# Windowed attention with a gated feed-forward layer: one unit's outputs and the next unit's scores in one visit to TensorE

## The chip, the cores and the metric

The kernel runs on one core of a Trainium2 chip. Its engines are TensorE (PE in the profile; PEld is its weight load), VectorE (DVE), ScalarE (ACT), GpSimd (POOL) and SyncE (SP), which issues the DMAs. The metric is the device time of one execution in microseconds, lower is better; the time of a kernel is the median of its runs.

## The reference

All in float32. Attention over 8 x 8 heads of 576 tokens with head size 64, each token seeing itself and the 63 tokens before it; then a gated layer over all 4608 tokens.

```python
scores = scale * np.matmul(q, k.transpose(0, 1, 3, 2))
rel = pos[:, None] - pos[None, :]
mask = (rel >= 0) & (rel < 64)
scores = np.where(mask, scores, -1000000000.0)
scores = scores - np.max(scores, axis=-1, keepdims=True)
attn = np.exp(scores)
attn = attn / (np.sum(attn, axis=-1, keepdims=True) + 1e-09)
out = np.matmul(attn, v)
x = out.transpose(0, 2, 1, 3).reshape(4608, 512)
gate = 1.0 / (1.0 + np.exp(-(x @ w_gate)))      # w_gate, w_val: 512 x 1536
y = gate * (x @ w_val) @ w_out                  # w_out: 1536 x 512
```

## The kernel before

The tokens are cut into 12 tiles of 384. A tile's attention is 4 units, one for each pair of heads, and a unit (t, p) goes through three stages, each a short visit to PE between long matmuls:

- `stage_a`, scores: 24 matmul records (12 instructions) of 64x64 weights write the scores of the pair's heads into two PSUM banks `s0` and `s1`. Per head and block, DVE takes masked row minima (L211), ACT the exp (L216), DVE sums up and inverts (L222, L223), and POOL scales (L225, giving `p`).
- `stage_b`: 6 transposes of `p` into two banks `pp` (L233), copied out by ACT as `pT` (L238).
- `stage_c`, outputs: 24 records with 128x64 weights (L248) into one bank `oo`, which ACT copies out as `xf` (L255; for tiles 0 and 1 it is split in two parts instead).

PSUM has 8 banks. Six have names of their own, three for even and three for odd s (`psum(s, i)`), and belong to the feed-forward part; the other two are the pool `ps_a` with tag `a`, which from the third tile on serves `s0`, `s1`, `pp` and `oo` in turn. All these tiles have 384 columns, and a bank holds 512, so a quarter of each stays free.

The feed-forward part has a first stretch (tiles 0 and 1, plain matmuls `up`, in rotating banks `h_bank`, and `down`), beside which the attention of tiles 2 and 3 runs and the weights are converted. Then come phases s = 1 to 5, each for tiles 2s and 2s+1 together, by a Strassen scheme: for k = 0 to 5 and m = 0 (gate), 1 (value) there are 7 `product`s n = 0 to 6, each of 6 matmuls of 384 columns (L438) into bank 0, 1 or 2 of the phase: n = 0 and 4 use bank 0, n = 1, 3 and 5 bank 1, n = 2 and 6 bank 2. Here is what leaves these banks, and lets PE write them again:

- n = 0: ACT copies the bank to `p1` (L449). n = 1: DVE adds `p1` to bank 1, giving `u`. n = 3: DVE forms `u` from bank 1 and `c` from bank 2. n = 5: `c` from bank 1. n = 6: `c` from bank 2 (all L444).
- With m = 0 a gate is made of each `c`, and of bank 0 itself after n = 4: ACT's Relu (L292), Tanh (L293) and Exp (L294), and on DVE an abs (L295) and a product (L297). With m = 1 DVE multiplies by the gates (L476, L481).

Behind n = 2, 4 and 6 a `down` (3 matmuls of 512 columns, L347) of the k before is put in where there is one; k = 0 has none, and the second half of k = 1 hardly any. When the products are done, the second tile's downs follow (`last_tile`). Beside phase s the attention of phase s+1's tiles runs, 8 units; phase 5 has none. Products are numbered by slots, 14 for each k.

What stands where on PE is written by hand: events are put with a time, sorted, and PE keeps that program order (`pe`). The order on DVE, ACT, POOL and SP is set by a scheduler that simulates the program when it is built, and each engine works through its queue in order. `q` and `k` of a unit have one buffer each, `v` two, the weights of the products (`W`) seven, each for two products; all loads are issued by SP.

The times of the stages beside a phase, before (the number is the slot behind which a stage stands):

```python
for n in range(2 * NP):
    for f, d in zip(range(3), (0, 6, 8)):
        fill.setdefault(21 * (n // 2) + (2, 11)[n % 2] + d, []).append((f, *unit(s + 1, n)))
```

Of the kernel before, what the change touches and what calls it, by code (L numbers as in the profile page):

```python
# [26 lines left out]
def attn_ffn(ctx: ExitStack, tc: tile.TileContext, qT, kT, vN, w_gate, w_val, w_out, out):  # L27
# [159 lines left out]

    def stage_a(t, p):
        qt, kt = ld.pop((t, p))
        g0 = order[t] * UT  # L190
# [9 lines left out]
        for h in range(2):  # L200
            if t < 2 and (NP * t + p) % 3 == 2:
                pt = mp.tile([P, TT], F32, name=f"p{h}_{t}_{p}", tag=("hh", "hl")[h], bufs=3)
                pt = pt.rearrange("p (u c) -> p u c", u=UP)
            else:
                pt = ap.tile([P, UP, P], F32, name=f"p{h}_{t}_{p}", tag="p", bufs=4)
            mn = sm.tile([P, UP], F32, name=f"mn{h}_{t}_{p}", tag="mn")
            rs = sm.tile([P, UP], F32, name=f"rs{h}_{t}_{p}", tag="rs")
            for u in range(UP):
                key = [int((g0 + 2 * u + s) % SEQ == 0) for s in range(2)]
                key = tuple(key[::-1] if h else key)  # L210
                nc.vector.tensor_tensor_reduce(out=pt[:, u, :], in0=sc[h][:, u, :], in1=masks[key],  # L211
                                               op0=ALU.add, op1=ALU.min, scale=-SCALE, scalar=3.0e38,
                                               accum_out=mn[:, u:u + 1])
                with table_order() if t < 4 else nullcontext():
                    sums = {} if t < 2 and h else {"accum_out": rs[:, u:u + 1]}
                    exp = nc.scalar.activation(pt[:, u, :], pt[:, u, :], AF.Exp, bias=mn[:, u:u + 1],  # L216
                                               scale=-1.0, **sums)
                if t < 4:
                    chain.append(exp.ins)
            if not sums:  # L220
                nc.vector.reduce_sum(out=rs, in_=pt, axis=mybir.AxisListType.X)
            nc.vector.tensor_scalar_add(out=rs, in0=rs, scalar1=1e-9)  # L222
            nc.vector.reciprocal(out=rs, in_=rs)  # L223
            eng = nc.vector if t == 3 and p % 2 else nc.gpsimd
            eng.tensor_mul(out=pt, in0=pt, in1=rs.unsqueeze(2).broadcast_to([P, UP, P]))  # L225
            st[(t, p, h)] = pt
# [14 lines left out]
    def stage_c(t, p):  # L241
        oo = bank(t, p, "o", f"oo_{t}_{p}").rearrange("p u c -> p (u c)")
        vt = vts.pop((t, p))
        pT = [st.pop((t, p, h)) for h in range(2)]
        for U in range(UT):
            for h in range(2):
                half = (U % 2) ^ h
                pe(nc.tensor.matmul(oo[h * BLK:(h + 1) * BLK, U * BLK:(U + 1) * BLK],  # L248
                                    vt[:, U, h * BLK:(h + 1) * BLK],
                                    pT[h][:, U // 2, half * BLK:(half + 1) * BLK], start=True, stop=True))  # L250
        if t < 2:
            xs[(t, p)] = x_split(oo, f"{t}_{p}", 4 * t + p, nc.vector)
        else:
            xf[(t, p)] = xp.tile([P, TT], F32, name=f"xf_{t}_{p}", tag=f"xf{4 * (t % 2) + p}")
            nc.scalar.copy(xf[(t, p)], oo)  # L255
# [426 lines left out]
```

## Time and profile before

| | before |
|---|---|
| median of 3 runs | 1029.6 us (1028.73 to 1029.66) |
| profiled execution | 1027.79 us, span 1026.0 us |
| granted PE clock, mean | 0.991 |
| busy PE / PEld / DVE / ACT / POOL | 988.4 / 884.8 / 660.3 / 526.3 / 264.5 us |
| DMA | 221.51 MB, mean 216 GB/s |

Busy time is the union of an engine's instructions. Matmuls are pipelined: a matmul's start is measured and its end modelled, so that consecutive ones overlap in the listing, and what a matmul takes of the queue is read from start to start. PE counts matmul records: each fp32 instruction of the attention makes two.

### The profile page before, as it was taken

How to read it: one execution, taken by the hardware profiler on the slowest of the kernel's cores; microseconds unless marked ns; L12 is line 12 of the kernel's file. 1: busy time of each engine (PE TensorE's matmuls, PEld its weight loads, DVE VectorE, ACT ScalarE, POOL GpSimd, SP SyncE). 2: the span in 40 equal slices, each digit the busy share in tenths (PEclk: the TensorE clock that was granted, in tenths of full speed). 3: DMA queues.
4: the chain of work that ended last, by engine and by line, in shares of the span. 5: the costliest groups of instructions: out<-in, count | busy, mean ns of one | idle time of the engine just before them, and what ended most of it. 6: DMA issues, size and time to landing. Idle time of an engine off the chain costs nothing.

```text
span 1026.0 us, 19846 instructions
## 1 busy us (share of the span) xinstructions
PE 988.4 (96%) x6984; PEld 884.8 (86%) x6984; DVE 660.3 (64%) x1810; ACT 526.3 (51%) x1409; POOL 264.5 (26%) x287
## 2 busy tenths in 40 slices
PE   5799999998999999999999999999999999999998
PEld 4688999788899888989988989988989988899996
DVE  6499987836676665666665776676666677344542
ACT  6687976735566544544453654454545544311122
POOL 4200101676762231122113221214112124010100
PEclk8899999999999999999999999999999999999999
DMA  9599985989999733767661776761677662476500
GB/s 302 198 304 376 342 303 189 334 294 342 368 315 329 216 109 111 241 211 223 202 197 34 238 240 199 224 199 49 215 225 212 211 189 84 131 226 195 197 31 32
DMA packets 126244, 221.51 MB, mean 216 GB/s; under 512 B 9409, under 2 KB 82625, under 8 KB 126145
## 3 DMA queue, kind: packets, MB, share of 16 engines
q1 hardware_dynamic: 126144, 220.24, 65.6%
q8 instruction: 56, 0.92, 0.4%
q14 instruction: 44, 0.35, 0.1%
HBM read 178.52 MB, written 41.68 MB: 215 GB/s over the span
## 4 chain that ended last, share of the span: by engine, by line
PE 74%; DMA 7%; DVE 6%; ACT 6%; POOL 3%; issue 3%; SPq 1%; POOLq 0%; DVEq 0%; ACTq 0%
PE pr L438 40%; PE y L347 23%; PE oo L248 3%; PE s L197 3%; PE ph L283 2%; ACT p L216 2%; PE pp L233 2%; DMA hd<-hh 1%; DVE w L122 1%; DMA a<-w32d 1%; DMA w32d<-w 1%; DVE w L124 1%; DMA q<-in_qT_dram 1%; POOL ws L144 1%; DMA out_dram<-yo 1%
## 5 line engine op out<-in xcount | busy, mean ns | idle before, releaser
L438 PE MATMUL pr<-x_T,wt 128*128 128x384 f32 x1440 | 288.3, 340 | 5.1 <-DVE c L444 2.8
L438 PEld LDWEIGHTS pr<-x_T,wt 128*128 128x128 f32 x1440 | 251.0, 188 | 21.1 <-DVE u L444 5.4
L347 PE MATMUL y<-w,hh 128*128 128x512 f32 x804 | 250.6, 392 | 0.3 <-DVE w L144 0.2
L438 PE MATMUL pr<-x_B,wt 128*128 128x384 f32 x1080 | 221.9, 342 | 0.2
L438 PEld LDWEIGHTS pr<-x_B,wt 128*128 128x128 f32 x1080 | 188.7, 188 | 7.9 <-ACT g L293 1.3
L225 POOL TENSOR_TENSOR p<-p,rs 128x384 f32<-128x384 f32 x92 | 79.4, 865 | 406.4 <-DVE rs L223 365.6
L347 PEld LDWEIGHTS y<-w,hh 128*128 128x128 f32 x804 | 148.4, 188 | 22.2 <-ACT hh L312 1.4
L347 PE MATMUL y<-w,hl 128*128 128x512 f32 x402 | 158.6, 394 | 0.7 <-DVE hl L316 0.7
L444 DVE TENSOR_TENSOR u<-pr,p 128x384 f32<-128x384 f32 x120 | 66.7, 556 | 132.3 <-PE pr L438 128.6
L216 ACT ACTIVATE p<-p,mn 128x128 f32<-128x128 f32 x288 | 110.5, 392 | 79.0 <-DVE mn L211 78.7
L316 POOL TENSOR_TENSOR hl<-h,hh 128x384 fp32r<-128x384 f32 x60 | 64.7, 1078 | 240.8 <-DVE hh L314 220.8
L283 PE MATMUL ph<-x,w 128*128 128x384 f32 x576 | 107.6, 339 | 1.1 <-DVE x L260 0.5
L283 PEld LDWEIGHTS ph<-x,w 128*128 128x128 f32 x576 | 99.5, 188 | 4.2 <-issue 1.2
L347 PEld LDWEIGHTS y<-w,hl 128*128 128x128 f32 x402 | 75.3, 187 | 19.4 <-DVE hl L316 3.2
L211 DVE CUSTOM_DVE_ANT_0 p<-s,m 128x128 f32<-128x128 f32 x288 | 64.7, 286 | 34.8 <-PE s L197 29.3
L449 ACT COPY p<-pr 128x384 f32<-128x384 f32 x60 | 28.4, 473 | 90.1 <-PE pr L438 83.5
L444 DVE TENSOR_TENSOR c<-pr,u 128x384 f32<-128x384 f32 x120 | 66.7, 556 | 12.3 <-PE pr L438 6.1
L238 ACT COPY pT<-pp 128x384 f32<-128x384 f32 x96 | 42.2, 480 | 50.2 <-PE pp L233 50.0
L248 PEld LDWEIGHTS oo<-pT,v 128*64 128x64 f32 x1152 | 40.8, 142 | 29.7 <-ACT pT L238 19.9
L316 DVE TENSOR_TENSOR hl<-hb,hh 128x384 fp32r<-128x384 f32 x60 | 39.1, 663 | 40.5 <-ACT hh L312 38.5
L248 PE MATMUL oo<-pT,v 128*64 128x64 f32 x1152 | 48.7, 231 | 15.8 <-ACT pT L238 15.6
L297 DVE SCALAR_TENSOR_TENSOR g<-g,e 128x384 f32<-128x384 f32 x96 | 52.8, 562 | 7.8 <-ACT e L294 5.4
(73 smaller groups left out, 1204.1 us busy)
## 6 DMA issues: line engine op xcount, KB each, us to landing
wt<-wd SPq DMA_DIRECT2D x210, 512.0 KB, 4.3
v<-in_vN_dram SPq DMA_DIRECT2D x48, 384.0 KB, 4.8
...
k<-in_kT_dram SPq DMA_DIRECT2D x48, 224.0 KB, 4.5
...
```

The source lines that it names most:

```text
L197: pe(nc.tensor.matmul(sc[h][half * BLK:(half + 1) * BLK, u, :], qt[h * BLK:(h + 1) * BLK, U * BLK:(U + 1) * BLK], kt[h * BLK:(h + 1) * BLK ...
L211: nc.vector.tensor_tensor_reduce(out=pt[:, u, :], in0=sc[h][:, u, :], in1=masks[key], op0=ALU.add, op1=ALU.min, scale=-SCALE, scalar=3.0e3 ...
L216: exp = nc.scalar.activation(pt[:, u, :], pt[:, u, :], AF.Exp, bias=mn[:, u:u + 1], scale=-1.0, **sums)
L225: eng.tensor_mul(out=pt, in0=pt, in1=rs.unsqueeze(2).broadcast_to([P, UP, P]))
L238: nc.scalar.copy(pT, pp)
L248: pe(nc.tensor.matmul(oo[h * BLK:(h + 1) * BLK, U * BLK:(U + 1) * BLK], vt[:, U, h * BLK:(h + 1) * BLK], pT[h][:, U // 2, half * BLK:(half ...
L283: pe(nc.tensor.matmul(ph, l, r, start=i == 0, stop=i == len(prs) - 1))
L297: nc.vector.scalar_tensor_tensor(out=g, in0=g, scalar=1.0, in1=e, op0=ALU.add, op1=ALU.mult)
L316: return eng.tensor_sub(out=h_lo, in0=h32, in1=h_hi.bitcast(F32))
L347: pe(nc.tensor.matmul(yb[y], l, r, start=first and n == 0, stop=last and n == 2))
L438: pe(nc.tensor.matmul(ps, l, r, start=new and i == 0, stop=i == len(prs) - 1, skip_group_check=not new))
L444: nc.vector.tensor_add(out=o, in0=ps, in1=a)
```

## The change

From the third tile on, unit n's `stage_c` and unit n+1's `stage_a` become one visit, `stage_ca`; a stretch's first unit keeps its own `stage_a`, and its last its own `stage_c`. The outputs no longer have a bank: their three blocks of 128 columns go into the free quarters of the two score banks of the next unit and of a third bank, `spare` (beside products the bank of product n = 0, in the first stretch the last but one of the `up` banks). ACT copies them out in three parts: the third bank's block ahead of the softmax, the second score bank's block ahead of it too, and the first score bank's block between the two heads. Scores now stand at slots 5, 12, 26, 33, 47, 54, 68 and 75, that is always behind product 5 of a group, with m = 0 at 5, 33, 47 and 75 (k = 0, 2, 3, 5), and the transposes 5 or 9 slots later. The loop below replaces the one quoted above.

```diff
+    def a_bank(nm):
+        return ps_a.tile([P, UP + 1, P], F32, name=nm, tag="a")
...
     def stage_a(t, p):
+        sc = [bank(t, p, f"s{h}", f"s{h}_{t}_{p}") for h in range(2)]
+        scores(t, p, sc)
+        for h in range(2):
+            softmax(t, p, h, sc[h])
...
+    def stage_ca(done, t, p):
+        sc = [a_bank(f"s{h}_{t}_{p}") for h in range(2)]
+        oo = [sc[0][:, UP, :], sc[1][:, UP, :], spare(t, p)[:, TT:TT + P]]
+        outputs(*done, oo)
+        scores(t, p, sc)
+        x = xf_tile(*done).rearrange("p (u c) -> p u c", u=UP)
+        nc.scalar.copy(x[:, 2, :], oo[2])
+        nc.scalar.copy(x[:, 1, :], oo[1])
+        softmax(t, p, 0, sc[0])
+        nc.scalar.copy(x[:, 0, :], oo[0])
+        softmax(t, p, 1, sc[1])
...
+    def spare(t, p):
+        if t // 2 > 1:
+            return tmp["first"]
+        return psum(1, 0, f"sp_{t}_{p}") if (t, p) == unit(1, 2 * NP - 1) else hbanks[-2]
...
-            for n in range(2 * NP):
-                for f, d in zip(range(3), (0, 6, 8)):
-                    fill.setdefault(21 * (n // 2) + (2, 11)[n % 2] + d, []).append((f, *unit(s + 1, n)))
+            for n, i in enumerate((5, 12, 26, 33, 47, 54, 68, 75)):
+                scores_at(i, s + 1, n)
+                fill[i + (9 if n in (1, 3, 5) else 5)] = (1, *unit(s + 1, n))
+            fill[82] = (2, *unit(s + 1, n))
```

`scores`, `softmax` and `outputs` are the old bodies of the stages, cut out as functions. In total ACT has 70 copies more; the other engines issue the same instructions as before. Lines move: L211 becomes L220, L216 L225, L248 L269, L444 L482, L449 L487, and the three copies of `stage_ca` are L281, L282 and L284.

PE before, phase 3, k = 0, m = 1 (`pr_1_3_0` is a bank of that group's products, behind its name the tile number; `oo_0` the outputs of unit (8, 0), `s_8_2` the scores of unit (8, 2)):

```order
L438 MATMUL pr_1_3_0_7270<-x_T_3_1_7068,wt_0_5_7038 128x384 x3
L248 MATMUL oo_0_7312<-pT_8_0_7283,v_0_7083 64x64
L248 MATMUL oo_0_7312<-pT_8_0_7289,v_0_7083 64x64
...
L438 MATMUL pr_1_3_0_7259<-x_B_3_0_6978,wt_0_5_7038 128x384 x3
L438 MATMUL pr_1_3_0_7259<-x_B_3_1_7085,wt_0_5_7038 128x384 x3
L197 MATMUL s_8_2_7341<-k_2_7254,q_2_7253 64x128
L197 MATMUL s_8_2_7342<-k_2_7254,q_2_7253 64x128
...
L438 MATMUL pr_1_3_0_7270<-x_T_3_0_6992,wt_0_6_7066 128x384 x3
```

And PE now at the same unit (outputs carry the names of the banks that they share):

```order
L476 MATMUL pr_1_3_0_7292<-x_T_3_1_7108,wt_0_6_7090 128x384 x3
L269 MATMUL s_8_2_7362<-pT_8_0_7326,v_0_7132 64x64
...
L269 MATMUL s_8_2_7363<-pT_8_0_7332,v_0_7132 64x64
L269 MATMUL pr_1_3_0_7281<-pT_8_0_7326,v_0_7132 64x64
...
L204 MATMUL s_8_2_7362<-k_2_7276,q_2_7275 64x128
L204 MATMUL s_8_2_7363<-k_2_7276,q_2_7275 64x128
...
L476 MATMUL pr_1_3_0_7301<-x_B_3_0_7027,wt_0_6_7090 128x384 x3
```

The product that stood between outputs and scores is gone from there, and both stand behind product 5.

ACT before, at the phase's first unit (8, 0), scores behind product 2 (`p_8_0` is the softmax's tile, `e` and `g` belong to gates, `p_0_3_0` and `p_1_3_0` are the copies p1 of m = 0 and m = 1):

```order
L449 COPY p_0_3_0_7131<-pr_0_3_0_7124 128x384
L216 ACTIVATE p_8_0_7165,rs_8_0_7167<-p_8_0_7165,mn_8_0_7166 128x128 x3
L216 ACTIVATE p_8_0_7177,rs_8_0_7179<-p_8_0_7177,mn_8_0_7178 128x128 x3
L292 ACTIVATE e_6_7202<-c_0_3_0_7199 128x384
L293 ACTIVATE g_6_7201<-c_0_3_0_7199 128x384
L292 ACTIVATE e_0_7215<-pr_0_3_0_7124 128x384
L293 ACTIVATE g_0_7214<-pr_0_3_0_7124 128x384
...
L292 ACTIVATE e_6_7230<-c_0_3_0_7227 128x384
L449 COPY p_1_3_0_7266<-pr_1_3_0_7259 128x384
```

ACT now, the whole stretch between the two copies p1 but for its first rows:

```order
L328 ACTIVATE g_0_7198<-pr_0_3_0_7148 128x384
L329 ACTIVATE e_6_7186<-e_6_7186 128x384
L328 ACTIVATE g_6_7213<-c_0_3_0_7211 128x384
L329 ACTIVATE e_0_7199<-e_0_7199 128x384
L225 ACTIVATE p_8_0_7236,rs_8_0_7238<-p_8_0_7236,mn_8_0_7237 128x128 x2
L327 ACTIVATE e_6_7214<-c_0_3_0_7211 128x384
L225 ACTIVATE p_8_0_7236,rs_8_0_7238<-p_8_0_7236,mn_8_0_7237 128x128
L225 ACTIVATE p_8_0_7248,rs_8_0_7250<-p_8_0_7248,mn_8_0_7249 128x128 x3
L329 ACTIVATE e_6_7214<-e_6_7214 128x384
L487 COPY p_1_3_0_7288<-pr_1_3_0_7281 128x384
```

The six exps, which stood ahead of the gates of products 3 to 5, now stand behind most of them and right ahead of the next p1; ahead of the rows shown are p1 of m = 0 and the Relu and Tanh of product 3 and the Relu of product 4.

DVE now, the same place (`c_0_3_0_7211` is c of product 5, `c_0_3_0_7266` that of product 6, `u_1_3_0` the next group's u):

```order
L482 TENSOR_TENSOR c_0_3_0_7211<-pr_0_3_0_7157,p_0_3_0_7155 128x384
L330 TENSOR_SCALAR g_6_7185<-g_6_7185 128x384
L330 TENSOR_SCALAR g_0_7198<-g_0_7198 128x384
L220 ISA p_8_0_7236,mn_8_0_7237<-s_8_0_7222,m_86 128x128
...
L332 SCALAR_TENSOR_TENSOR g_6_7185<-g_6_7185,e_6_7186 128x384
...
L330 TENSOR_SCALAR g_6_7213<-g_6_7213 128x384
L332 SCALAR_TENSOR_TENSOR g_0_7198<-g_0_7198,e_0_7199 128x384
L482 TENSOR_TENSOR c_0_3_0_7266<-pr_0_3_0_7166,u_0_3_0_7164 128x384
...
L332 SCALAR_TENSOR_TENSOR g_6_7213<-g_6_7213,e_6_7214 128x384
L482 TENSOR_TENSOR u_1_3_0_7299<-pr_1_3_0_7292,p_1_3_0_7288 128x384
```

Before, the row minima (L211) of this unit stood ahead of product 3's u and c:

```order
L211 ISA p_8_0_7177,mn_8_0_7178<-s_8_0_7152,m_86 128x128
L211 ISA mn_8_0_7178 128x1
L444 TENSOR_TENSOR u_0_3_0_7197<-pr_0_3_0_7135,p_0_3_0_7131 128x384
L222 TENSOR_SCALAR rs_8_0_7167<-rs_8_0_7167 128x3
L444 TENSOR_TENSOR c_0_3_0_7199<-pr_0_3_0_7144,u_0_3_0_7197 128x384
```

Now they stand between c of product 5 and c of product 6.

More of the change, by code (lines that the diff above doesn't have):

```diff
@@ L199, in stage_a @@
                                      kt[h * BLK:(h + 1) * BLK, U * BLK:U * BLK + P], start=True, stop=True))
[L200 to L226, printed above, removed]
@@ new lines, in softmax @@
+    def softmax(t, p, h, sc):
+        g0 = order[t] * UT
+        if t < 2 and (NP * t + p) % 3 == 2:
+            pt = mp.tile([P, TT], F32, name=f"p{h}_{t}_{p}", tag=("hh", "hl")[h], bufs=3)
+            pt = pt.rearrange("p (u c) -> p u c", u=UP)
+        else:
+            pt = ap.tile([P, UP, P], F32, name=f"p{h}_{t}_{p}", tag="p", bufs=4)
+        mn = sm.tile([P, UP], F32, name=f"mn{h}_{t}_{p}", tag="mn")
+        rs = sm.tile([P, UP], F32, name=f"rs{h}_{t}_{p}", tag="rs")
+        for u in range(UP):
+            key = [int((g0 + 2 * u + s) % SEQ == 0) for s in range(2)]
+            key = tuple(key[::-1] if h else key)
+            nc.vector.tensor_tensor_reduce(out=pt[:, u, :], in0=sc[:, u, :], in1=masks[key],
+                                           op0=ALU.add, op1=ALU.min, scale=-SCALE, scalar=3.0e38,
+                                           accum_out=mn[:, u:u + 1])
+            with table_order() if t < 4 else nullcontext():
+                sums = {} if t < 2 and h else {"accum_out": rs[:, u:u + 1]}
+                exp = nc.scalar.activation(pt[:, u, :], pt[:, u, :], AF.Exp, bias=mn[:, u:u + 1],
+                                           scale=-1.0, **sums)
+            if t < 4:
+                chain.append(exp.ins)
+        if not sums:
+            nc.vector.reduce_sum(out=rs, in_=pt, axis=mybir.AxisListType.X)
+        nc.vector.tensor_scalar_add(out=rs, in0=rs, scalar1=1e-9)
+        nc.vector.reciprocal(out=rs, in_=rs)
+        eng = nc.vector if t == 3 and p % 2 else nc.gpsimd
+        eng.tensor_mul(out=pt, in0=pt, in1=rs.unsqueeze(2).broadcast_to([P, UP, P]))
+        st[(t, p, h)] = pt
@@ L426, in product @@
         if new:
-            tmp[b] = psum(s, b, f"pr{b}_{m}_{s}_{k}")[:, :TT]
+            bk = psum(s, b, f"pr{b}_{m}_{s}_{k}")
+            tmp[b] = bk[:, :TT]
+            if n == 0:
+                tmp["first"] = bk
         ps = tmp[b]
@@ L510, in attn_ffn @@
         t, p = divmod(n, NP)
-        for f, d in zip(stages, (0, 10.6 - n // 7 * 2.2, 12.2)):
+        for f, d in zip(stages[:3], (0, 10.6 - n // 7 * 2.2, 12.2)):
             put(A0 + 3.6 * n + d, 6, f, t, p)
```

54 lines of the change are left out of this document (30 added, 24 removed).

## The prediction

> **What bounds the kernel now.** I read the page first, then the windows of the four stretches that carry attention and products together, then the PE timeline of two visits, and then ACT, DVE and PE around the places where PE waits. The page's busy times and chain, and the windows (stretch, PE busy, PEld, DVE, ACT, POOL):
> ```profile
> PE 988.4 (96%) x6984; PEld 884.8 (86%) x6984; DVE 660.3 (64%) x1810; ACT 526.3 (51%) x1409; POOL 264.5 (26%) x287
> PE 74%; DMA 7%; DVE 6%; ACT 6%; POOL 3%; issue 3%; SPq 1%; POOLq 0%; DVEq 0%; ACTq 0%
> ...
> 551.00:713.00 162.00, 161.14 (x1155) 143.94 (x1155) 106.55 (x300) 81.33 (x236) 35.82 (x36) 1.00 0.60 187
> ```
> PE is the bound: in a phase of 162.0 us it is busy 161.1, while DVE has 106.6 and ACT 81.3. So two things count: what PE itself spends on a visit of small matmuls, and the few places where the other engines, idle on average, are late for a PSUM bank. A busy PE hides switching costs, since ends of matmuls are modelled; I take them from starts. The PE timeline (start, duration, idle before in brackets):
> ```profile
> 510.16 1.23 PE L438 MATMUL pr<-x_T,wt 128*128 128x384 f32 x6
> 511.32 0.92 PE L248 MATMUL oo<-pT,v 128*64 128x64 f32 x24
> 512.17 1.31 PE L438 MATMUL pr<-x_B,wt 128*128 128x384 f32 x6
> 513.32 0.63 PE L347 MATMUL y<-w,hh 128*128 128x512 f32 x2
> 513.78 0.40 PE L347 MATMUL y<-w,hl 128*128 128x512 f32 x1
> 514.11 0.89 PE L197 MATMUL s<-k,q 64*64 64x128 f32 x24
> 514.92 1.31 PE L438 MATMUL pr<-x_T,wt 128*128 128x384 f32 x6
> 516.07 1.20 PE L438 MATMUL pr<-x_B,wt 128*128 128x384 f32 x6
> 517.11 0.63 PE L347 MATMUL y<-w,hh 128*128 128x512 f32 x2
> 517.57 0.40 PE L347 MATMUL y<-w,hl 128*128 128x512 f32 x1
> 517.81 1.22 PE L438 MATMUL pr<-x_B,wt 128*128 128x384 f32 x6
> 518.87 2.24 PE L438 MATMUL pr<-x_T,wt 128*128 128x384 f32 x12
> ...
> 521.41 0.40 PE L347 MATMUL y<-w,hl 128*128 128x512 f32 x1
> 522.23 1.32 PE L438 MATMUL pr<-x_T,wt 128*128 128x384 f32 x6 [0.41 <-DVE u L444]
> 523.39 0.82 PE L233 MATMUL pp<-ident,p 128*128 128x128 f32 x6
> 523.96 1.29 PE L438 MATMUL pr<-x_B,wt 128*128 128x384 f32 x6
> ```
> Undisturbed, six product matmuls last 1.04 us (516.07 to 517.11; 1.06 behind a down) and the last matmul of a down 0.24 (517.57 to 517.81). Before outputs six last 1.16 (510.16 to 511.32): entry 0.10. The outputs last 0.85 (to 512.17), and the six behind them 1.15: exit 0.11. Scores: entry 0.33 - 0.24 = 0.09, 0.81 of work, exit 0.11. A visit of outputs thus costs 1.06, one of scores 1.01, together 2.07.
>
> The same timeline has the waits of a phase: 0.82 instead of 0.24 at 521.41, so 0.58, for DVE's u. Two more:
> ```profile
> 567.96 2.57 PE L438 MATMUL pr<-x_B,wt 128*128 128x384 f32 x12
> 570.37 1.21 PE L438 MATMUL pr<-x_T,wt 128*128 128x384 f32 x6
> ...
> 600.96 0.82 PE L233 MATMUL pp<-ident,p 128*128 128x128 f32 x6
> 602.17 1.31 PE L438 MATMUL pr<-x_T,wt 128*128 128x384 f32 x6 [0.39 <-DVE c L444]
> ```
> Twelve last 2.41 instead of 2 x 1.04, and the transposes 1.21 instead of 0.57 (523.39 to 523.96): 0.33 and 0.64. A phase waits about 1.5 us in all.
>
> **The visit merged.** 7 of 8 units in each of five stretches (tiles 2 and 3, and phases 1 to 4) get one visit for two: 35. The same 24 + 24 matmul records run; one entry and one exit go, if scores follow outputs without a gap of their own. That junction stands in the trace once:
> ```profile
> 198.26 1.29 PE L248 MATMUL oo<-pT,v 128*64 128x64 f32 x24 [0.22 <-ACT pT L238]
> 199.48 0.43 PE L197 MATMUL s<-k,q 64*64 64x128 f32 x2
> ```
> The scores start 0.07 before the modelled end of the outputs (199.55), as products do at 512.17 (512.24). So a merged visit costs 0.10 + 0.85 + 0.81 + 0.11 = 1.87, and saves 0.20: **35 x 0.20 = 7.0 us**. [...] The one junction in the trace speaks for 0.20, and I take it.
>
> **Copies.** An output of 384 columns becomes three copies of 128: 70 ACT instructions more. The nearest rows are 373 and 478 ns for 256 and 384 columns, 392 for an exp of 128:
> ```profile
> L255 ACT COPY xf<-oo 128x384 f32<-128x384 f32 x40 | 19.1, 478 | 60.5 <-PE oo L248 60.4
> L353 ACT COPY yo<-y 128x256 f32<-128x256 f32 x3 | 1.1, 373 | 5.1 <-PE y L347 5.1
> L216 ACT ACTIVATE p<-p,mn 128x128 f32<-128x128 f32 x288 | 110.5, 392 | 79.0 <-DVE mn L211 78.7
> ```
> The straight line through the copies gives 0.27 (bounds 0.10 and 0.39); a unit's copies grow from 0.48 to 0.81 us, under a phase of which ACT is busy half. It costs where ACT is late, below.
>
> **Where the visits now stand.** Before, scores stood behind products 2 or 4 of a group; now each stands behind product 5, and with m = 0 the gate work of products 3 to 5 is ahead of the softmax on ACT and DVE. Their steps, start to start:
> ```profile
> 567.49 0.51 ACT L292 ACTIVATE e<-c 128x384 f32<-128x384 f32 x1
> 567.90 0.52 ACT L293 ACTIVATE g<-c 128x384 f32<-128x384 f32 x1
> ...
> 571.39 0.46 ACT L449 COPY p<-pr 128x384 f32<-128x384 f32 x1
> ...
> 565.04 0.28 DVE L211 CUSTOM_DVE_ANT_0 p<-s,m 128x128 f32<-128x128 f32 x1
> 565.25 0.28 DVE L211 CUSTOM_DVE_ANT_0 p<-s,m 128x128 f32<-128x128 f32 x1
> 566.10 0.55 DVE L444 TENSOR_TENSOR u<-pr,p 128x384 f32<-128x384 f32 x1
> 566.68 0.56 DVE L444 TENSOR_TENSOR c<-pr,u 128x384 f32<-128x384 f32 x1
> ```
> ACT takes 0.41 for a gate step and 0.39 for an exp; DVE 0.21 for a row minimum (L211) and 0.58 for an add (566.10 to 566.68).
>
> The worst place is a phase's first unit: k = 0, where no downs stand between the products. Time 0 is the phase's first matmul, products end at 1.05, 2.1 and so on, product 5 at 6.25, the scores at 7.16, product 6 at 8.3. ACT, in the order shown ahead: product 3's c is ready at 5.55, seven gate steps to 8.45, two exps 9.25, a Relu 9.65, four exps 11.2, an Exp 11.6, the copy p1 of the next group 12.1. DVE: c of product 5 at 7.05, two abs behind ACT to 7.8, two row minima 8.2, g times e 8.8, four minima 9.6, abs and g times e 10.6, and only then c of product 6, 11.2. PE wants that bank (2) for product 2 of the next group at 10.4: a wait of 0.8. Then p1 at 12.1 and, behind another g times e, u at 13.2, which frees bank 1 for product 3, wanted at 12.3: a wait of 1.0. **1.8 us a phase**, bounds 0.3 (what the first unit waits now) and 2.5.
>
> The other visits with m = 0 have downs of 0.70 (513.32 to 514.11, less the entry of 0.09) as slack. By the same steps u comes 0.1 late behind k = 2 (transposes on PE give 0.57 more room), 0.4 behind k = 3, and 0.7 behind k = 5, where a split of x for the next phase is queued on ACT ahead of p1: 1.2. Visits with m = 1 have no gates, and c and u come about 1 us early: nothing. The three waits of now (1.5) stand at visits that are gone. So a phase loses 1.8 + 1.2 - 1.5 = 1.5, four phases **6.0 us**.
>
> **Covered.** The third block of outputs goes where product 0's bank has its free quarter; PE waits for that bank's last reader, which ends 0.3 us ahead in the count above, and the copy out has at least a product (1.0 us) before the bank is written again. On SP the loads of q and k, single-buffered, wait for the unit before and hold up weight loads queued behind them:
> ```profile
> v<-in_vN_dram SPq DMA_DIRECT2D x48, 384.0 KB, 4.8
> k<-in_kT_dram SPq DMA_DIRECT2D x48, 224.0 KB, 4.5
> ```
> Units are now 7 products (at least 7.3 us) apart in pairs, against a landing of 4.5: hidden, and weights are 7 tiles, 14 products, ahead. If landing took 3 us more, each close pair would wait. Transposes come 5 products (5.2 us; with k above 0 two downs more, 6.6) behind scores, where 6 products (and the two downs, 7.6) stood. The softmax of a phase's first unit now ends 4.8 us behind its scores:
> ```profile
> 564.70 1.34 PE L438 MATMUL pr<-x_T,wt 128*128 128x384 f32 x6
> ...
> 568.68 0.83 POOL L225 TENSOR_TENSOR p<-p,rs 128x384 f32<-128x384 f32 x1 [0.38 <-DVE rs L223]
> ```
> With the gates ahead it ends at 13.0 by the count above, 5.8 behind the scores, and the transposes come at 14.3 because product 3 has waited: hidden, with 1.3 to spare. If POOL were busy elsewhere, PE would wait there. With tiles 2 and 3 ACT and DVE are loaded with weight conversion, and I count no change but the merge. In phase 1 PE waits once 1.8 us for pT, which POOL's and ACT's weight sums hold up:
> ```profile
> PE oo L248 <- ACT pT L238: 2.2, 2, 1.8
> ```
> I take the same again.
>
> **Sum.** -7.0 + 6.0 = -1.0. The profiled execution took 1027.8 (span 1026.0 and 1.8 around it); the sum makes it 1026.8. The median of the runs is 1.8 higher, 1029.6, so 1028.6. A difference under 0.2% (2.1 us) can't be told from none.
>
> **Rivals.**
> Faster: ACT and DVE keep up. A gate step is 0.41 only when queued, and a wait in front of one product can absorb the next one's. If new waits only equal the old ones, the merge is left, 1029.6 - 7.0 = 1022.6; for it speaks that ACT is busy half the phase, against it the 0.58 at 522.23, which is this very mechanism.
> Slower: the copy out of a score bank. DVE's minima of the second head now wait for ACT's copy of the outputs in the same bank, and ACT has gates ahead of it at the 16 visits with m = 0. By the steps above the copy just precedes the minima. If it is 0.4 us later at each, c of product 6 and the banks behind it move by as much: 16 x 0.4 = 6.4, 1035.0; it decides from 0.2 us at each. [...]
> [...]
>
> **Chances.** The forecast, no difference, 0.36; faster 0.34; the bank wait 0.18 and the dear junction 0.12, both slower, 0.30. The range reaches from the full merge to the bank wait, 1023 to 1035; the forecast alone runs from 1027.5 to 1031.6 by the bounds of 1.8 (-6.0 to +2.8) cut at what can be told.
>
> **What would show it.** Right: from a product through outputs and scores to the next product 1.66 us from start to start; in phases 2 to 4 PE waiting near 10 us behind the phase's start for DVE's c and then u, 1.8 in all; no waits at 41 and 123 us behind it. Wrong: those waits under 0.5 (faster), DVE's L220 waiting for ACT's L282 at most visits (slower), a gap between outputs and scores, or PE waiting for pp behind POOL's p.

## The result: slower by half a per cent

| | before | changed |
|---|---|---|
| median | 1028.41 us (10 runs, 1025.48 to 1029.66) | 1033.62 us (10 runs, 1030.65 to 1035.87) |
| profiled execution | 1027.79 us, span 1026.0 | 1030.65 us, span 1028.9 |
| ratio to before | | 1.0056, 95% interval 1.0042 to 1.0069 |

The changed kernel is slower, where no difference was forecast. The busy line of the page after, and behind it the window of 162 us whose line was shown of before (PE, PEld, DVE, ACT, POOL):

```profile
PE 983.7 (96%) x6984; PEld 884.9 (86%) x6984; DVE 662.8 (64%) x1810; ACT 530.8 (52%) x1479; POOL 263.0 (26%) x287
```

```profile
551.00:713.00 162.00, 159.80 (x1153) 143.63 (x1152) 105.45 (x299) 82.22 (x250) 35.05 (x37) 1.00 0.59 187
```

PE is busy 4.7 us less in a span that is 2.9 us longer: it saved something, and it waits more. Where, is read from four rows of the PE timeline in each kernel: the first down of tile 0, and the first products of phases 1, 3 and 4. Before:

```profile
62.77 0.50 PE L347 MATMUL y<-w,hh 128*128 128x512 f32 x1
...
228.83 1.23 PE L438 MATMUL pr<-x_B,wt 128*128 128x384 f32 x6
...
560.65 1.23 PE L438 MATMUL pr<-x_B,wt 128*128 128x384 f32 x6
722.29 1.23 PE L438 MATMUL pr<-x_B,wt 128*128 128x384 f32 x6
```

and changed:

```profile
62.69 0.50 PE L382 MATMUL y<-w,hh 128*128 128x512 f32 x1
...
229.42 1.23 PE L476 MATMUL pr<-x_B,wt 128*128 128x384 f32 x6
...
562.56 1.23 PE L476 MATMUL pr<-x_B,wt 128*128 128x384 f32 x6
724.89 1.23 PE L476 MATMUL pr<-x_B,wt 128*128 128x384 f32 x6
```

The "way" (first down to first product, with the attention of tiles 2 and 3 beside it) takes 166.7 instead of 166.1, though 7 of its visits are merged (1.4 us of the 7.0 forecast); phase 3 takes 162.3 instead of 161.6. The table has these differences of starts for all kernels run.

| kernel | way | phase 1 | 2 | 3 | 4 | ratio to before (95%) |
|---|---|---|---|---|---|---|
| before | 166.1 | 170.2 | 161.6 | 161.6 | 161.7 | 1 |
| changed | 166.7 | 170.9 | 162.3 | 162.3 | 162.0 | 1.0056 (1.0042 to 1.0069) |
| after_same | 166.0 | 171.3 | 162.2 | 162.4 | 162.0 | 1.0042 (1.0028 to 1.0056) |
| up_only | 165.7 | 170.1 | 161.8 | 161.7 | 161.7 | 1.0033 (1.0021 to 1.0046) |
| phase_only | 165.7 | 173.2 | 162.0 | 162.0 | 162.1 | 1.0045 (1.0033 to 1.0057) |
| copy_last | 165.8 | 171.3 | 162.3 | 162.3 | 162.1 | 1.0050 (1.0036 to 1.0064) |
| one_copy | 164.5 | 173.0 | 162.8 | 162.8 | 162.7 | 1.0057 (1.0042 to 1.0072) |
| first_at_2 | 166.8 | 170.6 | 160.8 | 160.8 | 160.9 | 1.0013 (1.0001 to 1.0025) |
| slots_moved | 165.5 | 173.4 | 163.1 | 163.2 | 163.2 | 1.0078 (1.0061 to 1.0094) |
| slots_old | 164.9 | 171.3 | 161.5 | 163.3 | 161.7 | 1.0027 (1.0016 to 1.0038) |
| slots_new | 165.0 | 167.6 | 159.7 | 159.7 | 159.7 | 0.9924 (0.9910 to 0.9937) |
| slots_fix | 165.6 | 168.0 | 158.9 | 159.0 | 159.0 | 0.9918 (0.9900 to 0.9936) |
| late_pp | 166.7 | 170.2 | 162.3 | 162.5 | 162.1 | 1.0059 (1.0035 to 1.0083) |
| fix_late | 167.4 | 168.7 | 159.0 | 158.9 | 159.0 | 0.9934 (0.9921 to 0.9947) |
| less_pe | 164.0 | 171.8 | 161.7 | 161.7 | 161.7 | 1.0019 (1.0005 to 1.0033) |
| less_dve | 164.1 | 171.7 | 161.7 | 161.7 | 161.8 | 1.0002 (0.9990 to 1.0015) |
| less_both | 160.4 | 168.6 | 162.0 | 161.6 | 161.7 | 0.9944 (0.9929 to 0.9959) |

The traced execution is the fastest of the changed kernel's ten, so the traces explain 2.9 us and the medians differ by 5.2. In after_same, the same kernel again, the traced execution took 1031.03 us and the median of 6 was 1031.94. What the slower executions do, no trace shows, and that part stays open. The table leaves out the time up to the first down, which runs from 62.7 us (changed) to 65.7 us (first_at_2) in these traces.

**The merge itself works as forecast.** The PE timeline of a visit in phase 3 of the changed kernel (the third block of outputs stands in a product bank, so its tile reads `pr`):

```profile
631.04 1.23 PE L476 MATMUL pr<-x_T,wt 128*128 128x384 f32 x6
632.20 0.69 PE L269 MATMUL s<-pT,v 128*64 128x64 f32 x16
632.71 0.40 PE L269 MATMUL pr<-pT,v 128*64 128x64 f32 x8
633.04 0.89 PE L204 MATMUL s<-k,q 64*64 64x128 f32 x24
633.86 1.14 PE L476 MATMUL pr<-x_B,wt 128*128 128x384 f32 x5
```

From the outputs to the next product it is 633.86 - 632.20 = 1.66 us, the forecast figure. The outputs still last 0.84, so no gap shows at the junction to the scores, and a visit saves 0.20.

**The phases give it back in waits.** Rows of PE around three of four places in phase 3 (562.56 is its start; the fourth is at 639.8):

```profile
571.96 2.58 PE L476 MATMUL pr<-x_T,wt 128*128 128x384 f32 x12
575.63 1.32 PE L476 MATMUL pr<-x_T,wt 128*128 128x384 f32 x6 [1.09 <-DVE u L482]
...
617.44 0.40 PE L382 MATMUL y<-w,hl 128*128 128x512 f32 x1
618.05 1.14 PE L476 MATMUL pr<-x_T,wt 128*128 128x384 f32 x5 [0.22 <-DVE u L482]
...
685.00 0.40 PE L382 MATMUL y<-w,hl 128*128 128x512 f32 x1
686.15 1.32 PE L476 MATMUL pr<-x_T,wt 128*128 128x384 f32 x6 [0.76 <-DVE u L482]
```

Twelve matmuls from 571.96 last 3.67 instead of 2 x 1.04, so 1.6 of waiting (forecast 1.8): 0.33 in front of product 2, inside the first row, and 1.25 in front of product 3. Behind the three downs, where 0.24 is normal, it is 0.37, 0.24 and 0.91 (forecast 0.1, 0.4 and 0.7). The sum is 3.1, against 3.0. The lesson in reading: the bracket shows idle time by modelled ends (0.22 at 618.05), the starts show the whole loss (0.37).

**Tiles 2 and 3 give it back in two other waits.** Before, the second head's transposes waited for the scaled scores `p` once (rows of PE):

```profile
89.06 0.49 PE L233 MATMUL pp<-ident,p 128*128 128x128 f32 x3
91.29 0.55 PE L233 MATMUL pp<-ident,p 128*128 128x128 f32 x3 [1.74 <-POOL p L225]
```

Changed, at the same place and once more later, and a window behind the first wait:

```profile
88.77 0.49 PE L242 MATMUL pp<-ident,p 128*128 128x128 f32 x3
92.60 0.90 PE L242 MATMUL pp<-ident,p 128*128 128x128 f32 x3 [3.34 <-POOL p L234]
...
194.98 0.52 PE L242 MATMUL pp<-ident,p 128*128 128x128 f32 x3 [2.10 <-DVE p L234]
```

```profile
93.20:95.70 2.50, 2.50 (x10) 2.50 (x9) 2.47 (x6) 1.28 (x3) 0.00 (x0) 0.50 1.04 405
```

PE comes 0.3 earlier and waits 1.6 longer, and then it runs at a granted clock of 0.50 for 2.5 us; half of that, about 1.25, is the estimate of what it costs. In return two waits of before for `xf`, 2.2 us together, are not there. All brackets of the way add up to 5.5 us before and 6.5 now. So +1.0 for waits, +1.25 for the clock and -1.4 for the merge make +0.9, where +0.7 was measured. What `p` waited for stands on DVE, before:

```profile
87.68 0.16 DVE L222 TENSOR_SCALAR rs<-rs 128x3 f32<-128x3 f32 x1
...
89.81 0.16 DVE L223 RECIPROCAL rs<-rs 128x3 f32<-128x3 f32 x1
```

and changed:

```profile
89.78 0.16 DVE L231 TENSOR_SCALAR rs<-rs 128x3 f32<-128x3 f32 x1
89.86 0.55 DVE L351 TENSOR_TENSOR hl<-h,hh 128x384 fp32r<-128x384 f32 x1
90.32 0.68 DVE L124 CUSTOM_DVE_ANT_0 w<-raw,w 128x1024 uint16<-128x1024 uint16 x1
90.92 0.55 DVE L357 TENSOR_TENSOR h<-ph,g 128x384 f32<-128x384 f32 x1
91.39 0.16 DVE L232 RECIPROCAL rs<-rs 128x3 f32<-128x3 f32 x1
```

Two steps of 0.16 us on three numbers a row come 2.1 and 1.6 us later than before. They stand among the conversion of the weights (L124) and the hidden layer (L351, L357) in a queue without a gap.

### The profile page after: what moved, and what is told of

Read it like the earlier page. It is cut to its first block, busy times and chain, and to the rows that moved or that the text cites. A ratio compares the mean times of both kernels' runs of the same rounds, so it can differ in the third digit from the quotient of the medians.

```text
span 1028.9 us, 19920 instructions
## 1 busy us (share of the span) xinstructions
PE 983.7 (96%) x6984; PEld 884.9 (86%) x6984; DVE 662.8 (64%) x1810; ACT 530.8 (52%) x1479; POOL 263.0 (26%) x287
## 4 chain that ended last, share of the span: by engine, by line
PE 58%; ACT 7%; DVE 4%; issue 2%; DMA 0%; POOL 0%; DVEq 0%; ACTq 0%; POOLq 0%
PE pr L476 33%; PE y L382 21%; ACT p L225 3%; PE pp L242 2%; ACT g L328 1%; ACT e L327 1%; DVE u L482 1%; PE s L204 1%; ACT e L329 1%; PE s L269 1%; DVE c L482 1%; DVE g L332 1%; DMA out_dram<-yo 0%; PE oo L269 0%; PE pr L269 0%
## 5 line engine op out<-in xcount | busy, mean ns | idle before, releaser
L476 PE MATMUL pr<-x_T,wt 128*128 128x384 f32 x1440 | 284.8, 339 | 12.7 <-DVE u L482 10.4
L482 DVE TENSOR_TENSOR u<-pr,p 128x384 f32<-128x384 f32 x120 | 66.6, 555 | 148.4 <-PE pr L476 147.4
L351 POOL TENSOR_TENSOR hl<-h,hh 128x384 fp32r<-128x384 f32 x60 | 62.9, 1049 | 319.9 <-DVE hh L349 307.9
L225 ACT ACTIVATE p<-p,mn 128x128 f32<-128x128 f32 x288 | 111.3, 395 | 17.4 <-DVE mn L220 16.6
L220 DVE CUSTOM_DVE_ANT_0 p<-s,m 128x128 f32<-128x128 f32 x288 | 65.9, 285 | 11.1 <-PE s L204 5.5
L482 DVE TENSOR_TENSOR c<-pr,u 128x384 f32<-128x384 f32 x120 | 66.6, 555 | 7.9 <-ACT g L507 3.3
L327 ACT ACTIVATE e<-c 128x384 f32<-128x384 f32 x72 | 37.6, 523 | 59.0 <-DVE c L482 58.3
L487 ACT COPY p<-pr 128x384 f32<-128x384 f32 x60 | 28.3, 472 | 73.3 <-PE pr L476 72.6
L351 DVE TENSOR_TENSOR hl<-hb,hh 128x384 fp32r<-128x384 f32 x60 | 39.1, 663 | 40.7 <-ACT hh L347 40.2
L330 DVE TENSOR_SCALAR g<-g 128x384 int32<-128x384 int32 x96 | 42.3, 448 | 25.9 <-ACT g L328 25.9
L347 ACT CAST hh<-hb 128x384 fp32r<-128x384 f32 x60 | 30.0, 512 | 51.5 <-PE y L382 51.5
```

Source lines behind the costliest of these rows:

```text
L220: nc.vector.tensor_tensor_reduce(out=pt[:, u, :], in0=sc[:, u, :], in1=masks[key], op0=ALU.add, op1=ALU.min, scale=-SCALE, scalar=3.0e38, ...
L327: nc.scalar.activation(e, ph, AF.Relu, scale=-1.0)
L330: nc.vector.tensor_scalar(out=g.bitcast(I32), in0=g.bitcast(I32), scalar1=0x7FFFFFFF, scalar2=None, op0=ALU.bitwise_and)
L347: nc.scalar.copy(h_hi, h32)
L351: return eng.tensor_sub(out=h_lo, in0=h32, in1=h_hi.bitcast(F32))
L476: pe(nc.tensor.matmul(ps, l, r, start=new and i == 0, stop=i == len(prs) - 1, skip_group_check=not new))
```

## Experiments

Two theories for the phases: S, the places of the visits make the waits; M, the merge makes them (copies, bank). Two for tiles 2 and 3: A, other engines hold PE up there, so what PE saves is given back; B, it is all in the phases; later P, only the place of the transposes is at fault. One thing holds for all of them: the order on DVE, ACT, POOL and SP comes from the scheduler, so an edit of one line can move others, or move nothing.

**The kernel again, and its two halves.** after_same is the changed kernel.

> The changed kernel once more, for a second trace. Phases 2 to 4 should last 162.3, 162.3 and 162.0 us again with PE's waits at the same places (11 to 13, 55, 77 and 123 us into a phase). If the stretch before the first product varies between executions, the first product starts later than 229.4 here: the first trace is one of the fastest executions (1030.65, median 1033.62), so 1 to 4 us later. If all of the stretches are alike, it starts at 229.4 and the total is 1030.7.

Measured: the first product starts at 229.46, so nothing of the 1 to 4 us shows there; way 166.0, phases 162.2, 162.4 and 162.0, total 1031.03 in the trace. Phases 2 to 4 repeat to 0.1 us. The way varies by 0.7, and by 1.0 when copy_last is counted in, which turned out to be the same program (below).

up_only merges in tiles 2 and 3 alone, phase_only in the phases alone (the text on up_only speaks of 14 visits, a slip: they are 7, and its 227.4 is worked out with 7):

```diff
 # up_only: the loop beside the phases is the one of before
-            for n, i in enumerate((5, 12, 26, 33, 47, 54, 68, 75)):
-                scores_at(i, s + 1, n)
...
+            for n in range(2 * NP):
+                for f, d in zip(range(3), (0, 6, 8)):
...
 # phase_only: the loop of tiles 2 and 3 is the one of before
-        scores_at(i + 0.5 + (i < len(plan) and plan[i][0] == "down"), 1, n)
+        fill.setdefault(i + 0.5 + (i < len(plan) and plan[i][0] == "down"), []).append((0, *unit(1, n)))
...
```

> Merged visits in tiles 2 and 3 alone; the phases as before. Theory A (the weight conversion on ACT and DVE, not PE, sets the stretch of tiles 2 and 3, and what PE saves there comes back as waits for the softmax): first product at 229.4 to 232.5, no earlier than before's 228.8, phases 161.6, total 0.5 to 3.5 us above before. Theory B (all of the loss is in the phases, the merge is worth its 0.20 us in each of 14 visits... of which 7 a tile pair): first product near 227.4, total 1 us or more below before.

> Merged visits in the product phases alone; tiles 2 and 3 as before. Theory A: first product at 228.8 as before, phases 1 to 4 longer by 0.7, 0.65, 0.7 and 0.3 as in the trace of the changed kernel, total 2.3 us above before, so 2 to 3 us below the changed kernel. Theory B: 5 us above before, no better than the changed kernel.

Measured: up_only 1.0033, its first product at 229.40, as A says. Its first down is 1.0 later than before's, so the way is 165.7, 0.4 shorter, which is less than three traces of one program differ by. The phases are as before (161.7 and 161.8). So B falls for this half: 7 merged visits bring no more than 0.4 of their 1.4 us, and the kernel is not faster. phase_only 1.0045, 4.7 us by medians: that is what B had forecast (5), not A (2.3). Phases 2 to 4 lose 0.4 each, where A gave 0.65, 0.7 and 0.3, but phase 1 loses 3.0, where A gave 0.7. The halves do not add up to the whole (3.0 and 4.7 us against 4.4 to 5.2). Why phase 1, beside which the sums of weights are still made, loses so much in this kernel is not shown; neither theory had it. Of up_only's 3.0 us the trace has little: the traced execution took 1028.37, the median is 1030.54.

**The places alone.** slots_moved has the new places without the merge, outputs one product ahead of the next scores:

```diff
-            for n, i in enumerate((5, 12, 26, 33, 47, 54, 68, 75)):
-                scores_at(i, s + 1, n)
-                fill[i + (9 if n in (1, 3, 5) else 5)] = (1, *unit(s + 1, n))
...
+            v = (5, 12, 26, 33, 47, 54, 68, 75, 83)
+            for n in range(2 * NP):
+                for f, i in ((0, v[n]), (1, v[n] + (9 if n in (1, 3, 5) else 5)), (2, v[n + 1] - 1)):
+                    fill.setdefault(i, []).append((f, *unit(s + 1, n)))
```

> The new places alone, in the phases alone: scores behind products 5, 12, 26, 33, 47, 54, 68 and 75, transposes as in the changed kernel, the outputs one product ahead of the next scores, in a visit of their own with one copy. Theory S: the waits of the changed kernel (1.25 near 13 us into a phase, 0.4, 0.2 and 0.9 at 55, 77 and 123) without the merge's saving: phases 161.64 - 1.65 + 3.6 = 163.6, plus up to 0.3 for outputs only one product behind their transposes at four places; total 8 us above before. Theory M: no such waits, phases at 161.6 or less.

PE rows of slots_moved (565.27 is the start of its phase 3):

```profile
565.27 1.23 PE L476 MATMUL pr<-x_B,wt 128*128 128x384 f32 x6
...
574.70 2.58 PE L476 MATMUL pr<-x_T,wt 128*128 128x384 f32 x12
578.37 0.98 PE L476 MATMUL pr<-x_T,wt 128*128 128x384 f32 x4 [1.09 <-DVE u L482]
...
689.06 0.40 PE L382 MATMUL y<-w,hl 128*128 128x512 f32 x1
690.00 1.32 PE L476 MATMUL pr<-x_T,wt 128*128 128x384 f32 x6 [0.55 <-DVE u L482]
...
728.44 1.23 PE L476 MATMUL pr<-x_B,wt 128*128 128x384 f32 x6
```

A phase takes 728.44 - 565.27 = 163.2, 1.5 above before, with the same 1.6 of waiting at the first unit (578.37 - 574.70 = 3.67), though no visit of its phases is merged: theory S. The other waits are 0.22, 0 and 0.70, smaller than in the changed kernel by 0.15, 0.24 and 0.21, in all 0.6. So the changed kernel is slots_moved less 1.4 for the merge plus 0.6, which is 0.8 less; 162.3 - 163.2 = -0.9 was measured.

**One place.** first_at_2 is the changed kernel with the first unit's scores where they stood before; this visit has no outputs in either kernel:

```diff
-            for n, i in enumerate((5, 12, 26, 33, 47, 54, 68, 75)):
+            for n, i in enumerate((2, 12, 26, 33, 47, 54, 68, 75)):
-                fill[i + (9 if n in (1, 3, 5) else 5)] = (1, *unit(s + 1, n))
+                fill[i + (8 if n == 0 else 9 if n in (1, 3, 5) else 5)] = (1, *unit(s + 1, n))
```

> The changed kernel with one number other: a phase's first unit scored behind product 2, as before, instead of 5 (its transposes stay where they are, behind product 10). Theory S: the wait of 1.25 and its restart of 0.11 near 13 us go, the old one of 0.33 stands in place of the 0.33 near 10: phases 1.3 shorter, 161.0, total 4 to 5 us below the changed kernel, near before. Rival (the wait is only pushed on, to u or to the transposes): phases within 0.4 of 162.3.

```profile
563.70 1.23 PE L476 MATMUL pr<-x_B,wt 128*128 128x384 f32 x6
...
573.45 3.42 PE L476 MATMUL pr<-x_T,wt 128*128 128x384 f32 x18
...
724.53 1.23 PE L476 MATMUL pr<-x_B,wt 128*128 128x384 f32 x6
```

Eighteen matmuls in a row (PE rows of first_at_2) where PE waited 1.6 before; phases of 160.8 instead of 162.3 and a ratio of 1.0013 instead of 1.0056. One number undoes most of the loss. Its phases 2 to 4 are 0.8 to 0.9 shorter than those of before; that the kernel is no faster than before lies outside them, in its trace in a first down 2.9 us later and a way 0.7 longer.

**The copies.** copy_last puts L284 behind the second head's softmax; one_copy has one ACT copy of 384 columns between the heads and no other (the outputs' second and third blocks are left out):

```diff
 # copy_last
-        nc.scalar.copy(x[:, 0, :], oo[0])
         softmax(t, p, 1, sc[1])
+        nc.scalar.copy(x[:, 0, :], oo[0])
 # one_copy
-        nc.scalar.copy(x[:, 2, :], oo[2])
-        nc.scalar.copy(x[:, 1, :], oo[1])
         softmax(t, p, 0, sc[0])
-        nc.scalar.copy(x[:, 0, :], oo[0])
+        nc.scalar.copy(x, oo[0].unsqueeze(1).broadcast_to([P, UP, P]))
```

> The changed kernel with the copy of the outputs' first block behind the second head's softmax instead of ahead of it. Theory C (the copies on ACT delay the second head's exps, and so its row sums on DVE and the transposes): the wait for pp at 92.6 us falls from 3.5 to 1.9 or less, the first product starts 1.5 to 3 us earlier, total 2 to 3 us below the changed kernel. Theory A without the copies' part: that wait stays within 0.5 of 3.5 and the total within 1 us of the changed kernel. PE's waits at 11 to 13 us into a phase (1.25 and 0.22) stay in either case, since that visit has no outputs.

> The changed kernel with one ACT copy of 384 columns a visit instead of three of 128 (the first block of outputs three times; the other two blocks are not copied). Theory K (the three copies ahead of the exps make what is left, 0.6 a phase): the waits at 55, 77 and 123 us fall to those of slots_moved (0.22, 0, 0.71), the last downs no longer wait 0.27 for hl, phases 161.6 to 161.8. Rival (the 0.6 comes from the outputs' later place, not from the copies): phases 162.2 to 162.4 again. The wait of 1.25 stays in either case. The first product by theory A at 229 +- 0.7, whatever the copies do.

copy_last did not do what its text says. The scheduler put the third copy at the same place all the same. ACT in copy_last, where the copy is L285:

```profile
613.50 0.39 ACT L225 ACTIVATE p<-p,mn 128x128 f32<-128x128 f32 x1
...
613.89 0.24 ACT L285 COPY xf<-s 128x128 f32<-128x128 f32 x1
614.04 0.40 ACT L225 ACTIVATE p<-p,mn 128x128 f32<-128x128 f32 x1
```

In all 35 merged visits it stands ahead of the second head's exps, as in the changed kernel, and on every engine the two traces have the same instructions in the same order. So copy_last is a third trace of the changed kernel (1.0050; the wait at 92.5 is 3.06 by its bracket, phases 162.3), and theory C was not tested.

one_copy is worse in the phases, 162.8, where theory K gave 161.6 to 161.8 and the rival 162.2 to 162.4: neither came out. PE's waits at 55, 77 and 123 us are 0.73, 0.24 and 1.27, the first and last 0.36 above the changed kernel's. Its first product starts at 227.66, below the 229 +- 0.7 that theory A gave, and its way of 164.5 is the shortest with merged visits, so the copies may have a share there. The groups of ACT's copies, of the changed kernel and of one_copy:

```profile
L282 ACT COPY xf<-s 128x128 f32<-128x128 f32 x35 | 9.1, 260 | 10.8 <-PE s L204 10.7
L284 ACT COPY xf<-s 128x128 f32<-128x128 f32 x35 | 8.5, 244 | 0.0
L281 ACT COPY xf<-pr 128x128 f32<-128x128 f32 x28 | 7.3, 260 | 63.8 <-PE pr L269 63.8
```

```profile
L282 ACT COPY xf<-s 128x384 f32<-128x384 f32 x35 | 16.0, 457 | 0.0
```

L281 and L282 stand mostly where ACT is idle, waiting for the outputs and the scores (63.8 and 10.8 us of idle time in front of them). L284 has none in front, and the exp behind it starts 0.15 us after it; three such steps are 0.44 of the 0.60 by which the waits exceed those of slots_moved. In one_copy the step is 0.36, but at the visit ahead of the wait at 55 us the scheduler also put DVE's first row minimum behind a gate's product, so that the longer waits can't be put down to the copy alone. What makes the 0.6 stays open; a kernel without the third copy was not tried.

**Merged visits at better places.** slots_old has the old scores' places, slots_new and slots_fix have places chosen to keep clear of the gates; all three leave tiles 2 and 3 as before. In slots_old and slots_new some third blocks go into bank 0 between products 0 and 4, while that bank's sum is still to be added to, and the kernel's results come out different (relative error to the reference 0.168 and 0.167), so that only their times are read.

```diff
 # slots_old
+            for n, i in enumerate((2, 11, 23, 32, 44, 53, 65, 74)):
 # slots_new
+            for n, i in enumerate((2, 11, 23, 30, 39, 51, 58, 67)):
 # slots_fix
+            for n, i in enumerate((2, 11, 21, 29, 39, 49, 57, 67)):
 # all three: transposes 6 slots behind the scores
+                fill[i + 6] = [(1, *unit(s + 1, n))]
 # slots_fix: behind products 0 and 1 the third block goes to the last group's bank 2
-            return tmp["first"]
+            return tmp["first"] if tmp["n"] > 3 else tmp["last"]
```

> The merge alone, in the phases alone: merged visits where the scores stood before (products 2, 11, 23, 32, 44, 53, 65, 74 of a phase), outputs 1 to 4 products later than before. Theory S (the phases lose by the new places; the merge is worth 0.21 us in each of 7 visits): phases 2 to 4 last 161.64 - 1.46 = 160.2 us, PE still waiting near 41 and 123 us into a phase and no longer at 12 and 55; total about 4 x 1.5 = 6 us below before if phase 1 follows. Theory M (the merge itself makes the waits: three copies on ACT and the second head's minima behind one of them): new waits behind most visits, phases at or above 161.6, total at or above before.

> Merged visits, in the phases alone, at places chosen so that only three of the eight fall into a group with gates (m = 0), all of them behind its product 2, ahead of the gates: products 2, 11, 23, 30, 39, 51, 58, 67. Theory S: the waits at 41 and 123 us (0.74 and 0.58 with their restarts) go with the places behind product 4 of a gate group, the merge saves 1.46, the wait of 0.33 at the first unit stays: phases 161.64 - 1.46 - 1.3 = 158.9, total about 10 us below before. Theory M: phases no better than 161.6.

> As slots_new (merged visits in the phases alone, few of them among the gates), but no block of outputs goes into a bank whose sums are still to be added to: visits at products 2, 11, 21, 29, 39, 49, 57, 67; behind products 0 and 1 of a group (21, 29, 49, 57) the third block goes into bank 2 as the group before left it, else into bank 0. Theory S: as slots_new, 159.7 a phase or a little less (its wait of 0.65 at 36 us stood with the visit behind product 2 of a gate group; if it goes, 159.0), total 8 us below before. Rival: product 2 waits for ACT's copy out of bank 2, up to 0.5 at each of the four places: 161.5 a phase, no better than before.

slots_old gained nothing (161.5, 163.3, 161.7; S gave 160.2, M 161.6 or more). Its waits of PE from 399 to 723 us, two phases, show a cost that I had not counted:

```profile
PE pr L269 <- ACT g L328: 3.1, 4, 1.0
```

Behind product 4 of a gate group the third block waits for ACT's Relu and Tanh, which read bank 0 itself. These 1.5 us a phase eat the merge's 1.4. That is part of theory M, though by the bank and not by the copies, and the changed kernel avoids it by standing behind product 5. Phase 3 has in addition a wait of 0.9 for `u`. slots_new (159.7, where 158.9 was expected) and slots_fix (158.9, where 159.0 to 159.7 was expected) bear out S. A window of slots_fix, and the starts of its phases 2 and 3:

```profile
551.00:713.00 162.00, 161.91 (x1167) 146.89 (x1166) 103.53 (x299) 83.55 (x251) 35.62 (x36) 1.00 0.58 187
```

```profile
398.38 1.23 PE L479 MATMUL pr<-x_B,wt 128*128 128x384 f32 x6
557.30 1.23 PE L479 MATMUL pr<-x_B,wt 128*128 128x384 f32 x6
```

A phase takes 158.9, 2.7 less than before: 1.4 from the merge and the rest from the waits of before, of which the first unit's 0.33 is left. The median is 1019.36 us, a ratio of 0.9918 (0.9900 to 0.9936): this version beats both kernels.

**What sets the stretch of tiles 2 and 3.** Three cuts in the kernel before (what is left out stands in the expectations):

```diff
 # less_pe, in up
+        prs.pop()
 # less_dve, in conv_b
-        nc.vector.tensor_add(out=wi, in0=wi, in1=r32)
 # less_both: both
```

> The kernel before without the last of the twelve matmuls of every up product of tiles 0 and 1 (48 x 0.174 = 8.3 us of TensorE work less; the low half of one weight block is left out of the sums). Theory A (the conversion of the weights, not PE, sets that stretch): the first product of phase 1 starts within 1.5 us of 228.8, and what PE saves turns up as waits. Rival: PE sets it, and the first product starts 7 to 8 us earlier, near 221; then the merge's 2.8 us there should have been seen, and something else took them.

> The kernel before without one of DVE's steps of the weight conversion (the add of the low word, 36 x 0.68 = 24 us of DVE; the weights lack their low bits). Theory A1 (DVE's queue sets the stretch of tiles 2 and 3): the first product of phase 1 starts 4 us or more earlier than 228.8. Theory A2 (DMA, 0.96 to 0.81 busy there, sets it): within 1.5 us of 228.8. In the phases nothing changes, 161.6.

> The kernel before with both cuts: one of twelve matmuls of the up products of tiles 0 and 1 left out (8.3 us of PE), and the add of the low word in the weight conversion (24 us of DVE). Each alone shortened the way from the first down to the first product by 2 us (164.0 and 164.1 against 166.1). If PE and DVE hold each other up, the two together give more than the sum: 160 or less. If transfers or ACT set the stretch: 163 or more.

The first down and the first product on PE in less_both (the table has the way of the other two):

```profile
63.18 0.63 PE L347 MATMUL y<-w,hh 128*128 128x512 f32 x2
...
223.57 1.23 PE L438 MATMUL pr<-x_B,wt 128*128 128x384 f32 x6
```

8.3 us of PE work less, 7.3 of them in the way (42 of the 48 products), shorten it from 166.1 to 164.0, and phase 1 then takes 1.6 longer: 1.0019, nothing gained. 24 us of DVE work less: 164.1, 1.0002. Both: 160.4, just above the 160 of the text, but 5.7 less, more than 2.1 and 2.0 together, and this time it stays (0.9944). The six kernels with separate visits in tiles 2 and 3 and no such cut have ways of 164.9 to 166.1, 165.4 in the mean; against that mean the savings are 1.5, 1.4 and 5.1, and the reading is the same. Taken by the first product, as the texts do, less_pe (229.12) and less_dve (228.51) lie within 1.5 of 228.8, which is theory A for the one and A2, transfers, for the other; but if transfers alone set the stretch, less_both would have stayed at 163 or more. So neither PE nor DVE alone sets the stretch, nor do transfers alone: a saving on one comes back mostly as waits. That the merge's 1.4 us there (the text on less_pe says 2.8, the same slip) was lost in this way fits, but is not shown step by step. What share transfers (DMA 0.96 busy from 90 to 140 us before), ACT and the scheduler's new orders have in it was not separated.

late_pp moves the transposes of tiles 2 and 3 by half an up product, fix_late does so in slots_fix with merged visits in tiles 2 and 3:

```diff
-        fill[i + (3.5 if i + 3 < len(plan) and plan[i + 3][0] == "up" else 4)] = (1, *unit(1, n))
+        fill[i + (4 if i + 3 < len(plan) and plan[i + 3][0] == "up" else 4.5)] = (1, *unit(1, n))
```

> The changed kernel with the transposes of tiles 2 and 3 half an up product (2.1 us) later. Theory P (their place is at fault: PE waits there only because the normalised scores come late): the wait of 3.5 at 92 us falls to 1.4 or less and the one of 2.3 at 195 to nothing, no matmuls at half clock behind them, and from the first down to the first product of phase 1 it takes 163 to 164.5 us (changed kernel 166.7 and 166.0, before 166.1). Theory A (the stretch is set by the weights' conversion and transfers): PE waits as long elsewhere, and that stays at 165.5 to 167. Phases as in the changed kernel, 162.3.

> The places and banks of slots_fix in the phases, and in tiles 2 and 3 merged visits with the transposes half an up product later. Theory P: the phases at 159.0 and the first product 2 us earlier than in slots_fix, total 2 us below it, near 1017. Theory A: within 1 us of slots_fix or up to 1 us above.

The wait at 92 us is gone in late_pp, and PE stands still at the next gate instead (its PE row):

```profile
114.52 1.33 PE L318 MATMUL ph<-x,w 128*128 128x384 f32 x3 [2.50 <-ACT g L339]
```

Its way is 166.7 and its ratio 1.0059. fix_late is 1.2 us above slots_fix by medians, 0.2 more than A allowed, but the intervals of the two overlap. Theory P falls, and A is what is left.

## Why the prediction was wrong

**Visit merged, 35 x 0.20 = 7.0.** The size was right (1.66 us as forecast; no gap at the junction). The step failed in counting the 7 of tiles 2 and 3. The sentence "I count no change but the merge" took PE for the bound there because it is the bound in a phase. The way came out at 164.5 to 167.4 us in eight traces with merged visits (mean 166.2) and 164.9 to 166.1 in six with separate ones (mean 165.4). The row for it was at hand in the windows of before, DVE busy 46.72 of 50 us and DMA 0.96:

```profile
90.00:140.00 50.00, 48.25 (x360) 44.69 (x361) 46.72 (x115) 42.22 (x91) 5.22 (x5) 1.00 0.96 334
```

This step was to gain 1.4 us and lost 0.7 in the trace.

**New waits in a phase.** 1.8 + 1.2 was forecast and 3.1 measured. That place makes the largest wait was shown by first_at_2. That the sums agree is in part luck: of the first unit's 1.6, 0.33 stands in front of product 2, where 0.8 for `c` was forecast, and 1.25 in front of product 3, where 1.0 for `u` was. Of the old waits, 0.33 and 0.64 are gone. The 0.58 is not gone: before the same product, 123 us into the phase, now stands 0.91. The prediction had put down 0.7 there, and yet it named "no waits at 41 and 123 us" as a sign of being right.

The second step that failed is the size of what a phase loses, 0.1 = 1.5 - 1.4. What was left out: a wait costs another 0.1 in the matmul behind it (behind the wait at 575.63 us it takes 0.28 from start to start, those after it 0.17), 0.2 for two such matmuls more than before, and another 0.28 comes at a place that differs: in phase 2 in front of a product 42.8 us into it (0.52 behind a down where 0.24 is normal), in phase 3 in the last downs (32.17 us from its last product to phase 4, before 31.89), in phase 4 at neither. So phases 2 and 3 lose 0.7 each, and phases 1 to 4 lose 2.3 in the trace (0.66, 0.66, 0.68, 0.29) against 0.4.

**Sum.** -1.0 was forecast, -1.4 for tiles 2 and 3 and +0.4 for the phases; the trace has +0.7 and +2.3, less 0.1 for an earlier first down, +2.9. The other 2.3 us up to the medians' 5.2 are in no trace.

**Rivals.** The bank wait, which had most of the chance for slower, did not come. DVE's waits in the changed kernel have no row of L220 behind ACT's L282, only one for the scores and one at the kernel's start:

```profile
DVE p L220 <- PE s L204: 5.5, 11, 0.8
DVE p L220 <- POOL m L69: 5.5, 1, 5.5
```

The dear junction, whose 0.12 was an estimate, did not come either: no run shows a cost of its own for the change from outputs to scores, and in the changed kernel the outputs last 0.84 us up to the scores where they last 0.85 up to a product before. The case that did come, slower because PE is not the bound in one stretch and the merge does not cover the waits in the others, was not among the rivals, though both its parts stood in the text. One sign of being wrong did show it: PE waits for `pp` behind POOL's `p`, 3.34 us in tiles 2 and 3.
